# Decode attention on one core: two heads share each K and V tile with 64 KB rows, one V buffer, an in-place fold and block-diagonal probabilities

## The chip, the cores and the metric

The kernel runs on one core of a Trainium2 chip. The time is the device time of one execution, in microseconds (us). "The profile" is one profiled execution; its span (from the first to the last instruction) is some 1.7 us shorter than the device time of the same execution.

## The reference

One token goes through a block with adaptive layer norm: attention over a long cache, then a gated feed-forward network (FFN). What matters is the attention: 32 query heads, each with its own K and V of 16,384 keys by 128, all bfloat16.

```python
B, Sq, D = (1, 1, 640)
Hq, Hkv, Sk, Dh = (32, 32, 16384, 128)
...
h = _layernorm(x, axis=-1) * (1 + ca) + sa
q = (h @ wq).reshape(B, Sq, Hq, Dh).transpose(0, 2, 1, 3)
scores = jnp.einsum('bhqd,bhkd->bhqk', q, k) * Dh ** (-0.5)
p = _softmax(scores, axis=-1)
o = jnp.einsum('bhqk,bhkd->bhqd', p, v)
x = x + ga * (o.transpose(0, 2, 1, 3).reshape(B, Sq, Hq * Dh) @ wo)
# ... then the FFN: w_gate, w_up [640, 1728], w_down [1728, 640]
```

K and V are 268 MB of the 290 MB that one execution reads, and every byte is used once.

## The kernel before

Every head's K (4 MB) is laid over 128 partitions, so each partition gets 128 keys: one contiguous row of 32 KB. VectorE multiplies it by the query (spread over all partitions) and adds the two halves of the 128 products into `f1`; TensorE, with an identity matrix, adds further, down to eight partial sums a key, in PSUM (the memory that TensorE writes to); VectorE reduces those eight. Then maximum, exp, and PV (the probabilities times V) on TensorE. Two K slots and two V slots take turns. Every operation has a position number, and each engine runs its operations in the order of these numbers.

```python
kring = sb("kring", [128, 2, TT, 128], BF16)      # TT = 128 keys a partition
vring = sb("vring", [128, 2, TT, 128], BF16)
f1 = sb("f1", [128, TT, 64], BF16)
kv = lambda t, h: t[0, h].rearrange("(p t) d -> p t d", p=128)
# ... for each head h; s2 = h % 2; NH = 2 chunks, TH = 64
d_k[h] = plan.dma(qpos["k", h], kring[:, s2], kv(A_k, h), ("k", s2),
                  deps=[o_fold1[h - 2]] if h >= 2 else [], ...)
vdeps = [o_pvlast[h - 2]] if h >= 2 else [o_mod_a, o_mod_b, o_gbrmm]
# ... for each chunk c
o_mult[h] = op(DVE, base + 6.5 * c, ... tensor_tensor(out=ks, in0=ks, in1=qb, op=ALU.mult), ...)
o_fold1[h] = op(DVE, base + 6.5 * c + 4.4, ... tensor_tensor(
    out=f1h, in0=ks[:, :, 0:64], in1=ks[:, :, 64:128], op=ALU.add), ...)
# ... f_fold: eight matmuls with the identity; red, max, exp; then
def f_pv(e, s2=s2, sp=sp):
    for j in range(NJ):
        q4 = 32 * (j % 4)
        r = e.matmul(acc_ps[s2][q4:q4 + 32, :], lhsT=P_sb[:, sp, 4 * j:4 * j + 32],
                     rhs=vring[:, s2, 4 * j:4 * j + 4, :]..., start=(j < 4), stop=(j >= NJ - 4))
# ... acc (PSUM to SBUF), diag (picks the diagonal blocks out), on (divides by the sum), wo (output projection)
```

## Time and profile before

| | kernel before |
|---|---|
| time, median of 3 runs | 688.63 us (688.21 to 688.77) |
| span of the profiled run | 686.8 us |
| first transfer packet / last weight packet lands | 1.8 us / 682.7 us |
| DMA rate, 150 to 640 us | 430 GB/s |

First come lines of the page of the kernel before: the busy time of the engines, then the share of busy DMA engines (in tenths) and the GB/s in 40 equal slices, and the packets.

```profile
span 686.8 us, 7505 instructions
PE 350.9 (51%) x3320; PEld 174.7 (25%) x3320; DVE 482.4 (70%) x251; ACT 81.5 (12%) x308; POOL 51.3 (7%) x75
DMA  9999999999999999999999999999999999999996
DMA packets 12845, 290.96 MB, mean 424 GB/s; under 512 B 1354, under 2 KB 2060, under 8 KB 3724
```

No engine but the DMA is above 70%, and the DMA row is full until the last slice. The table of busy time by stretch says the same with numbers; its last two columns are the DMA share and GB/s.

```profile
core 0: us, PE busy (x) PEld busy (x) DVE busy (x) ACT busy (x) POOL busy (x), PEclk, DMA share, GB/s
50.00:100.00 50.00, 26.83 (x179) 11.56 (x179) 42.52 (x21) 6.61 (x25) 11.44 (x6) 0.71 1.00 430
100.00:105.00 5.00, 4.38 (x41) 1.55 (x40) 4.13 (x3) 0.60 (x1) 0.00 (x0) 0.82 0.99 426
105.00:110.00 5.00, 2.82 (x36) 2.13 (x34) 3.17 (x3) 1.52 (x6) 1.68 (x2) 0.86 0.97 419
150.00:640.00 490.00, 251.39 (x2061) 118.94 (x2061) 374.37 (x176) 58.89 (x221) 30.69 (x50) 0.69 1.00 430
```

The two big VectorE operations, from the groups of instructions (the numbers after the bar are total us and mean ns):

```profile
L425 DVE TENSOR_TENSOR kring<-kring,qbc_sb 128x8192 bf16<-128x8192 bf16 x64 | 283.0, 4422 | 94.4 <-DMA kring<-in_A_k_cache_dram 70.0
L427 DVE TENSOR_TENSOR f<-kring 128x4096 bf16<-128x4096 bf16 x64 | 146.7, 2292 | 2.2
```

And the end: first the chain of waits (start, duration, what), then three lines of the timeline.

```profile
653.02 28.72 DMA kring<-in_B_w_down_dram
681.79 0.73 PE psb L594 x16
684.44 0.33 DVE o_row L604
```

```profile
671.43 0.17 DVE L549 TENSOR_TENSOR h_col<-tt,mod_col 128x5 bf16<-128x5 f32 x1
676.77 2.24 PE L563 MATMUL psb<-h_col,wreg 128*128 128x1 bf16 x70 [2.52 <-DMA wreg<-in_B_w_up_dram]
684.79 0.63 SPq L71 DMA_DIRECT2D out_dram<-o_row  x1
```

The FFN's input `h_col` is ready at 671.4 us, but the "up" matmuls still wait 2.5 us for their weights, and after that the down weights are the last wait. The kernel is limited by transfers from the first packet to the last; only about 4 us at the end and 2 at the start are something else.

### The profile page before, as it was taken

Reading aid. Unit: us, or ns where it says so; the run is one execution under the profiler, and the core shown is the slowest. Engines: PE = TensorE matmul, PEld = TensorE weight load, DVE = VectorE, ACT = ScalarE, POOL = GpSimd, SP = SyncE. Lnnn points to the kernel's source line nnn. Section 1 sums busy time; section 2 is a strip of 40 time slices with the busy share of each in tenths; the row PEclk is TensorE's granted clock in tenths of the full one; section 3 lists DMA queues with packets and bytes.
Section 4 is the critical chain, followed back from the end, with each engine's and each line's share of the span. In section 5 each row is a group of like instructions: output and inputs, shape, how many; then the busy total and the mean of one; then the engine's idle time right before and its main releaser. Section 6 shows DMA issues by size and latency. Waiting matters only on the chain.

```text
span 686.8 us, 7505 instructions
## 1 busy us (share of the span) xinstructions
PE 350.9 (51%) x3320; PEld 174.7 (25%) x3320; DVE 482.4 (70%) x251; ACT 81.5 (12%) x308; POOL 51.3 (7%) x75
## 2 busy tenths in 40 slices
PE   1525665545655344655445456553445455565464
PEld 1501222222222122322122222321222122232143
DVE  0078888767778777768887677787777788877811
ACT  0100111111100011110111111100111011110010
POOL 0002222000000000000000000000000222200000
PEclk9997777666677676676777666775776566666755
DMA  9999999999999999999999999999999999999996
GB/s 387 409 434 427 433 434 435 426 433 430 431 420 441 430 427 428 430 429 434 431 433 430 430 427 431 427 434 428 433 436 418 438 428 428 428 429 430 425 421 238
DMA packets 12845, 290.96 MB, mean 424 GB/s; under 512 B 1354, under 2 KB 2060, under 8 KB 3724
## 3 DMA queue, kind: packets, MB, share of 16 engines
q1 hardware_dynamic: 12808, 290.48, 98.9%
q8 instruction: 26, 0.43, 0.3%
q14 instruction: 7, 0.06, 0.0%
q10 hardware_dynamic: 4, 0.00, 0.0%
HBM read 290.47 MB, written 0.00 MB: 423 GB/s over the span
## 4 chain that ended last, share of the span: by engine, by line
DMA 51%; DVE 41%; PE 6%; ACT 1%; issue 1%; SPq 1%; POOL 0%; DVEq 0%
DMA kring<-in_A_k_cache_dram 46%; DVE kring L425 26%; DVE f L427 14%; DMA kring<-in_B_w_down_dram 4%; PE psb L435 3%; PE psb L485 1%; SPq L71 1%; DVE S_sb L439 0%; ACT P_sb L450 0%; PE psb L465 0%; PE psb L594 0%; ACT R_sb L408 0%; POOL gm L446 0%; ACT qbc_sb L414 0%; PE psb L411 0%
## 5 line engine op out<-in xcount | busy, mean ns | idle before, releaser
L425 DVE TENSOR_TENSOR kring<-kring,qbc_sb 128x8192 bf16<-128x8192 bf16 x64 | 283.0, 4422 | 94.4 <-DMA kring<-in_A_k_cache_dram 70.0
L435 PE MATMUL psb<-f,ident 128*128 128x512 bf16 x512 | 177.6, 510 | 255.0 <-DVE f L427 254.9
L427 DVE TENSOR_TENSOR f<-kring 128x4096 bf16<-128x4096 bf16 x64 | 146.7, 2292 | 2.2
L435 PEld LDWEIGHTS psb<-f,ident 128*128 128x128 bf16 x512 | 56.4, 121 | 355.4 <-DVE f L427 275.2
L439 DVE TENSOR_REDUCE S_sb<-psb 128x64 f32<-128x512 f32 x64 | 44.0, 688 | 52.4 <-PE psb L435 52.4
L465 PE MATMUL psb<-vring,P_sb 128*32 128x512 bf16 x992 | 75.0, 455 | 9.2 <-DMA vring<-in_A_v_cache_dram 9.2
L485 PEld LDWEIGHTS psb<-sel,acc_sb 128*32 128x32 f32 (+1 forms) x920 | 59.8, 158 | 13.8 <-issue 11.9
L485 PE MATMUL psb<-sel,acc_sb 128*32 128x1 f32 (+1 forms) x920 | 62.0, 201 | 0.7 <-ACT acc_sb L470 0.7
L470 ACT ACTIVATE acc_sb<-psb 128x512 f32<-128x512 f32 x31 | 18.5, 597 | 355.7 <-PE psb L465 355.7
L446 POOL PARTITION_ALL_REDUCE gm<-pm x32 | 11.2, 351 | 533.4 <-DVE pm L443 515.3
L465 PEld LDWEIGHTS psb<-vring,P_sb 128*32 128x32 bf16 x992 | 26.6, 111 | 64.6 <-DMA vring<-in_A_v_cache_dram 28.1
L453 POOL PARTITION_ALL_REDUCE Ls<-rs x32 | 37.3, 1164 | 48.8 <-ACT P_sb L450 48.8
L411 PE MATMUL psb<-R_sb,ones_bf 128*128 128x128 bf16 x32 | 8.5, 266 | 35.8 <-ACT R_sb L408 35.2
L504 ACT ACTIVATE On<-psb,rl 32x4 bf16<-32x4 f32 (+1 forms) x32 | 8.2, 256 | 125.4 <-PE psb L485 120.7
L411 PEld LDWEIGHTS psb<-R_sb,ones_bf 128*128 128x128 bf16 x32 | 3.2, 101 | 39.8 <-ACT R_sb L408 39.8
L450 ACT ACTIVATE P_sb<-S_sb,nb 128x128 bf16<-128x128 f32 x32 | 12.9, 402 | 1.0
L408 ACT ACTIVATE R_sb<-ident,q_r 128x128 bf16<-128x128 bf16 x32 | 12.4, 387 | 0.0
L448 ACT ACTIVATE nb<-gm 128x1 f32<-128x1 f32 x32 | 6.4, 199 | 40.6 <-POOL gm L446 40.1
L540 DVE TENSOR_TENSOR tt<-attn_bf,mod_col 128x5 f32<-128x5 bf16 x1 | 0.2, 167 | 14.8 <-ACT attn_bf L539 14.8
L414 ACT ACTIVATE qbc_sb<-psb 128x128 bf16<-128x128 f32 x32 | 8.9, 277 | 11.5 <-PE psb L411 11.5
L512 PE MATMUL psb<-On,woring 128*128 128x1 bf16 x160 | 8.1, 179 | 3.9 <-ACT On L504 3.9
L443 DVE TENSOR_REDUCE pm<-S_sb 128x1 f32<-128x128 f32 x32 | 9.2, 286 | 1.1
(72 smaller groups left out, 85.6 us busy)
## 6 DMA issues: line engine op xcount, KB each, us to landing
kring<-in_A_k_cache_dram SPq DMA_DIRECT2D x32, 4096.0 KB, 25.4
vring<-in_A_v_cache_dram SPq DMA_DIRECT2D x31, 4096.0 KB, 35.3
wreg<-in_A_wq_dram SPq DMA_DIRECT2D x1, 5120.0 KB, 26.9
woring<-in_A_wo_dram SPq DMA_DIRECT2D x8, 640.0 KB, 26.6
vring<-in_w_mod_dram SPq DMA_DIRECT2D x1, 4800.0 KB, 14.3
vring<-in_A_v_cache_dram SPq DMA_DIRECT2D x4, 1024.0 KB, 12.5
wreg<-in_B_w_gate_dram SPq DMA_DIRECT2D x1, 2160.0 KB, 19.8
wreg<-in_B_w_up_dram SPq DMA_DIRECT2D x1, 2160.0 KB, 24.6
```

What stands on the lines that cost most here:

```text
L408: o_R[h] = op(ACT, base - 15.0 if h > 0 else 2.5, lambda e, h=h, s2=s2: e.activation(out=R_sb[:, s2], in_=ident[:], func=ACTF.Copy, scale= ...
L411: o_qbcmm[h] = op(PE, base - 14.8 if h > 0 else 2.7, lambda e, s2=s2: e.matmul(qbc_ps[s2], lhsT=ones_bf[:], rhs=R_sb[:, s2], start=True, s ...
L425: o_mult[h] = op(DVE, base + 6.5 * c, lambda e, ks=ks, qb=qb: e.tensor_tensor(out=ks, in0=ks, in1=qb, op=ALU.mult), deps=[d_k[h], o_qbc[h] ...
L427: o_fold1[h] = op(DVE, base + 6.5 * c + 4.4, lambda e, ks=ks, f1h=f1h: e.tensor_tensor(out=f1h, in0=ks[:, :, 0:64], in1=ks[:, :, 64:128], ...
L435: r = e.matmul(sh, lhsT=ident[:], rhs=f1h[:, :, GC * m:GC * (m + 1)], start=(m == 0), stop=(m == n - 1))
L439: reds.append(op(DVE, base + 15.0 + c, lambda e, s2=s2, sh=sh, c=c: e.tensor_reduce(out=S_sb[:, s2, c * TH:(c + 1) * TH], in_=sh, axis=AX. ...
L446: o_gm[h] = op(POOL, base + 17.3, lambda e, h=h: e.partition_all_reduce(gm[:, h:h + 1], pm[:, h:h + 1], channels=128, reduce_op=bass.bass_ ...
L450: o_exp[h] = op(ACT, base + 18.2, lambda e, h=h, s2=s2, sp=sp: e.activation(out=P_sb[:, sp, 0:TT], in_=S_sb[:, s2], func=ACTF.Exp, scale=S ...
L453: o_L[h] = op(POOL, base + 18.6, lambda e, h=h: e.partition_all_reduce(Ls[:, h:h + 1], rs[:, h:h + 1], channels=128, reduce_op=bass.bass_i ...
L465: r = e.matmul(acc_ps[s2][q4:q4 + 32, :], lhsT=P_sb[:, sp, 4 * j:4 * j + 32], rhs=vring[:, s2, 4 * j:4 * j + 4, :].rearrange("p a d -> p ( ...
L470: o_acc[h] = op(ACT, vbase + 3.0, lambda e, s2=s2: e.activation(out=acc_sb[:, s2, :], in_=acc_ps[s2][:], func=ACTF.Copy), deps=[o_pvlast[h ...
L485: r = e.matmul(dst, lhsT=blk, rhs=sel[:, i:i + 1], start=(i == 0), stop=(i == 3))
```

## The change

The intent: two heads (a pair) are one tile of 8 MB, 64 partitions a head, so each partition's row is one run of 64 KB, with half as many packets and half as many softmax chains. Beside two such K slots the kernel keeps one V buffer only; the fold writes into the K tile itself, the early and late weights borrow the tiles, and PV is cut into two halves that are placed among the next pair's folds. Each half of the partitions belongs to another head, so the probabilities are written as a block-diagonal matrix (columns of the other head are zero), and one PV pass serves both heads. The core of the diff:

```diff
-    kv = lambda t, h: t[0, h].rearrange("(p t) d -> p t d", p=128)
+    kv = lambda t, i: t[0, 2 * i:2 * i + 2].rearrange("h (p t) d -> (h p) t d", p=64)
-    vring = sb("vring", [128, 2, TT, 128], BF16)
-    f1 = sb("f1", [128, TT, 64], BF16)
+    kring = sb("kring", [128, 2, TP, 128], BF16)      # TP = 256
+    vbuf = sb("vbuf", [128, TP, 128], BF16)
 ... (wm_v, wq_v and the FFN weights are views of vbuf and of K slot 1)
+    order += [("k", NI - 2), ("k", NI - 1), ("v", NI - 3), ("v", NI - 2), ("wo", NI // 2 - 1), ("v", NI - 1)]
+    vt = [kring[:, 0] if i == NI - 2 else vbuf for i in range(NI)]
+    op_pos = []                                       # positions of PV half a, PV half b, diag
+    for i in range(NI):
+        nxt = T0 + (i + 1) * PERIOD                   # start of the next pair; its folds are at +6.9, +13.9, +20.9, +27.9
+        if i < NI - 3:
+            op_pos.append((nxt + 14.0, nxt + 21.0, nxt + 28.0))
+        elif i == NI - 3:
+            op_pos.append((nxt + PERIOD - 6.0, nxt + PERIOD - 5.0, nxt + PERIOD - 4.0))
 ... (the last two pairs)
+    o_f1 = op(DVE, base + 7.0 * c + 4.4, ... tensor_tensor(
+        out=ks[:, :, 0:64], in0=ks[:, :, 0:64], in1=ks[:, :, 64:128], op=ALU.add), deps=[o_mult[i]], ...)
+    o_exp[i] = op(ACT, ..., out=P_sb[half[b], sp, 0:2 * TP].rearrange("p (t b) -> p b t", b=2)[:, b, :], ...)
+    vdeps = [...] if i == 0 else [o_fold[i][-1]] if i == NI - 2 else [o_pvlast[i - 2 if last else i - 1]]
+    o_pva = op(PE, pva, lambda e, f=f_pv, j=jc[0]: f(e, 0, j), deps=[o_exp[i], d_v[i][0], ...])
+    o_pvb = op(PE, pvb, lambda e, f=f_pv, j=jc: f(e, j[0], j[1]), deps=[o_pva, ...])
```

## The prediction

> **What bounds the kernel now.** The DMA engines. The 40-slice page shows DMA at 9 in all slices but the last; the table of busy time by stretch gives a DMA share of 1.00 and 430 GB/s over 60 to 640 us. VectorE is busy 70%, TensorE 51%; neither sets the pace, as the queue is never empty (a K load takes 25.4 us to land, 9.7 of them its own transfer). The chain of waits says "DMA K 46%, VectorE 41%" only because it hops to whatever freed a buffer. Sum: 1.8 us to the first packet, 680 of transfers, 4.5 from the last weight packet to the end.
>
> **What the change does to that bound.** Bytes stay (290 MB); the row per partition goes from 32 KB to 64 KB. Packet records of the trace: 8 KB takes 312 ns, 17 KB 647, 32 KB 1215, 40 KB 1514: a line of 0.0367 ns/B (435 GB/s over 16 engines) plus about 10 ns a packet. The Trainium skill, "DMA: Bandwidth & Descriptors", "Where 436 GB/s comes from", gives 435 GB/s as the ceiling of the SBUF ports; the trace agrees, so only those 10 ns can be won. About 250 packets per engine disappear: an estimated 2.7 us, if a 64 KB row moves as one packet (three chances in four); nothing if it is cut in two.
>
> **What it removes off the critical path.** Half of the max and all-reduce bubbles (VectorE waits 4.9 us per head between last fold and next multiply; then about 5.5 per pair). VectorE per pair: 4 x (4.42 + 2.29) + 4 x 0.7 + 2 x 0.45 + wait = about 34 us against 39 of DMA. The in-place fold keeps 16-bit unit-step runs, so I expect 2.29 us again (the skill's "VectorE: DVE Perf Modes", "What auto-detection actually checks", asks for that). PV, diagonal and fold matmuls keep count and shape. All hidden.
>
> **What it adds.** One V buffer, and PV cut in two among the next pair's folds. In steady state the next V load is issued 30 us after its pair's multiply starts, 9 us before the queue runs dry: no loss. Only at the start is it late: the first K tile is twice as long, so VectorE starts at 47.6 us instead of 37.9, pair 1 at about 81, and the second half of PV of pair 0, after three folds of pair 1, ends at about 108.5; but the K tile of pair 2 has landed at 106.6. The queue is empty for about 3 us, once. By pair 3 VectorE has caught up. At the end the transfers keep their order, FFN weights last; the last PV chunk ends near 667.5 us as before and the up weights still land later, so the tail stays.
>
> **Sum.** 688.6 - 2.7 x 0.75 + 3 = about 689.5 us. Range 684 to 695. Within 2%: 0.92; faster 0.02; slower 0.06.
>
> **What would show it.** Packets of 65,536 bytes at about 2420 ns (else 32 KB at 1215). About 432 GB/s from 150 to 640 us. A stretch of 2 to 4 us without DMA near 106 to 110 us, the queue waiting for PV matmuls. 64 multiplies at 4.42 and 64 folds at 2.29 us.
>
> **What would make it wrong.** 64 KB rows moving slower (engines reading the same memory channels); the in-place fold losing its fast mode (4.5 us each: VectorE 43 us a pair, slower by about 60 us in all); stalls of the single V buffer in steady state (each counts 16 times); no stall at the start (then 686).

## The result, and the profile after

| | before | changed |
|---|---|---|
| time, median of 4 runs | 688.61 us | 689.53 us (688.09 to 689.80) |
| ratio to before, 95% interval | | 1.001 (0.9993 to 1.0027): the same |
| span of the profiled run | 686.8 us | 687.6 us |
| last weight packet lands | 682.7 us | 681.7 us |

Ratios here are the mean time of one kernel's runs over the mean of the other's runs of the same rounds, so they are not quite the ratios of the medians that are quoted. The total is what was predicted, to 0.1 us. But a sum can be right with wrong terms, so each term was looked up.

The page of the changed kernel, the same lines:

```profile
span 687.6 us, 7232 instructions
PE 352.1 (51%) x3264; PEld 169.6 (25%) x3264; DVE 484.0 (70%) x251; ACT 68.4 (10%) x245; POOL 26.5 (4%) x45
DMA  9999999999999999999999999999999999999995
DMA packets 8089, 290.92 MB, mean 423 GB/s; under 512 B 826, under 2 KB 1532, under 8 KB 3196
```

The packets fell by 37%, the bytes stayed. The mean rate did not rise, and the table of stretches shows why:

```profile
core 0: us, PE busy (x) PEld busy (x) DVE busy (x) ACT busy (x) POOL busy (x), PEclk, DMA share, GB/s
50.00:100.00 50.00, 22.78 (x82) 7.10 (x82) 45.67 (x21) 2.22 (x9) 3.56 (x2) 0.69 1.00 434
100.00:105.00 5.00, 2.80 (x28) 1.14 (x28) 5.00 (x3) 0.00 (x0) 0.00 (x0) 1.00 0.94 406
105.00:110.00 5.00, 1.48 (x22) 0.53 (x15) 4.97 (x3) 1.17 (x3) 0.00 (x0) 1.00 0.60 210
150.00:640.00 490.00, 257.19 (x2091) 119.02 (x2092) 372.29 (x172) 50.60 (x178) 14.97 (x25) 0.66 1.00 432
```

From 150 to 640 us the rate is 432 GB/s where it was 430, but from 105 to 110 us the DMA share falls to 0.60. (This view counts a packet whole in the stretch where it starts, so the share shows the place of a gap and only roughly its size.) The packet records of the trace give the first part exactly (ns of one packet):

| bytes of one packet | before | changed |
|---|---|---|
| 16,384 | | 612 median |
| 32,768 | 1215 median, 1218.8 mean (8064 of them) | 1214.5 median (128) |
| 65,536 | | 2420 median, 2427.0 mean (3968) |

Two packets of 32 KB take 2 x 1218.8 = 2437.6 ns and one of 64 KB takes 2427.0, so a pair of rows gains 10.6 ns. Each of the 16 engines moves 3968 / 16 = 248 of them: 2.6 us.

The second part is the gap. The timeline of the changed kernel, the transfer queue and TensorE around 100 us:

```profile
79.07 0.33 SPq L71 DMA_DIRECT2D kring<-in_A_k_cache_dram  x1
106.11 0.33 SPq L71 DMA_DIRECT2D vbuf<-in_A_v_cache_dram  x1
111.51 0.33 SPq L71 DMA_DIRECT2D kring<-in_A_k_cache_dram  x1
```

```profile
98.21 1.91 PE L482 MATMUL psb<-vbuf,P_sb 128*32 128x512 bf16 x32
102.32 1.90 PE L445 MATMUL psb<-kring,ident 128*128 128x512 bf16 x8 [2.20 <-DVE kring L438]
104.15 1.91 PE L482 MATMUL psb<-vbuf,P_sb 128*32 128x512 bf16 x32
```

The second half of PV of pair 0 (104.15 us) stands behind the third fold of pair 1 (102.32 us). When it is done, V of pair 1 may be loaded into the only V buffer: issued at 106.11 us, first packet at 107.06. The K tile in front of it had ended, engine by engine, between 104.8 and 106.6 us. So the 16 engines idled 1.7 us on average, but all of them at once only 0.45 us. This uneven end is what the Trainium skill leads one to expect ("DMA: Bandwidth & Descriptors", "Why a DMA increments its semaphore by 16 and not by 1": the engines of one transfer finish independently); the 1.8 us between first and last is this trace's number.

VectorE kept its two operations at their speed; the in-place fold costs the same 2292 ns:

```profile
L436 DVE TENSOR_TENSOR kring<-kring,qbc_sb 128x8192 bf16<-128x8192 bf16 x64 | 282.7, 4418 | 119.0 <-DMA kring<-in_A_k_cache_dram 111.4
L438 DVE TENSOR_TENSOR kring<-kring 128x4096 bf16<-128x4096 bf16 x64 | 146.7, 2292 | 2.2
```

The third part is at the end. The chain of waits of the changed kernel, from its last 50 us:

```profile
651.88 3.00 PE psb L482 x25
661.20 0.62 ACT P_sb L462 x2
663.95 3.57 PE psb L482 x32
676.43 0.18 DVE h_col L573
676.66 4.44 PE psb L587 x140
685.20 0.33 DVE o_row L628
```

There is no transfer in it any more; the last one of the whole chain is the V tile of pair 13, which landed at 625.4 us. The FFN's input is ready at 676.4 us, 5.0 us later than before; gate and up then run in one piece (140 matmuls, 4.44 us), as all their weights are there:

```profile
676.43 0.17 DVE L573 TENSOR_TENSOR h_col<-tt,mod_col 128x5 bf16<-128x5 f32 x1
676.66 4.43 PE L587 MATMUL psb<-h_col,kring 128*128 128x1 bf16 x140 [1.87 <-DVE h_col L573]
685.55 0.63 SPq L71 DMA_DIRECT2D out_dram<-o_row  x1
```

The transfers ended 1.0 us earlier than before and the output went out 0.8 us later: the tail grew by 1.8 us. Followed back, the delay starts here:

```profile
625.42 6.13 PE L482 MATMUL psb<-vbuf,P_sb 128*32 128x512 bf16 x64 [6.91 <-DMA vbuf<-in_A_v_cache_dram]
632.26 3.79 PE L508 MATMUL psb<-sel,acc_sb 128*32 128x1 f32 x64 [0.71 <-ACT acc_sb L491]
637.48 5.08 PE L445 MATMUL psb<-kring,ident 128*128 128x512 bf16 x16
640.88 0.69 DVE L449 TENSOR_REDUCE S_sb<-psb 128x64 f32<-128x512 f32 x1 [6.53 <-PE psb L445]
```

On TensorE, PV of pair 13 waits for its V tile, then its diagonal picks and the output projection follow, and only after all of that the first fold of pair 15 (the first eight of the 16 matmuls from 637.48 us), whose operands had been ready since 627.6 us (the fold on VectorE started at 625.39 and took 2.29). VectorE waits 6.5 us for that fold, and the exp of the last pair comes at 661.2 us, after its V had begun to land.

So my theory after the result: **A**, three terms nearly cancel: -2.6 us of packets, a gap at the start, a longer tail. Its rival **B**: nothing of this counts, the two kernels are equal because the bytes are equal and row size and small gaps do not matter; the early end and late end are noise. For the tail alone there is a second rival, **C**: the last pair's own work is longer (two heads, 64 matmuls and two outputs at the end).

### The profile page after: what moved, and what is told of

It reads as the page before. It is cut to its first block, busy times and chain, and to the rows that moved or that the text cites. A ratio compares the mean times of both kernels' runs of the same rounds, so it can differ in the third digit from the quotient of the medians.

```text
span 687.6 us, 7232 instructions
## 1 busy us (share of the span) xinstructions
PE 352.1 (51%) x3264; PEld 169.6 (25%) x3264; DVE 484.0 (70%) x251; ACT 68.4 (10%) x245; POOL 26.5 (4%) x45
## 4 chain that ended last, share of the span: by engine, by line
DMA 46%; DVE 36%; PE 12%; issue 3%; ACT 2%; another core or an unknown queue 1%; SPq 0%; POOL 0%; POOLq 0%; DVEq 0%
DMA kring<-in_A_k_cache_dram 38%; DVE kring L436 23%; DVE kring L438 10%; DMA vbuf<-in_A_v_cache_dram 7%; PE psb L445 4%; PE psb L508 3%; PE psb L482 2%; DVE S_sb L449 2%; PE psb L535 1%; ACT P_sb L462 1%; PE psb L587 1%; PE psb L618 0%; ACT On L527 0%; SPq L71 0%
## 5 line engine op out<-in xcount | busy, mean ns | idle before, releaser
L445 PE MATMUL psb<-kring,ident 128*128 128x512 bf16 x512 | 185.3, 528 | 251.5 <-DVE kring L438 251.4
L445 PEld LDWEIGHTS psb<-kring,ident 128*128 128x128 bf16 x512 | 58.3, 124 | 370.3 <-DVE kring L438 277.2
L438 DVE TENSOR_TENSOR kring<-kring 128x4096 bf16<-128x4096 bf16 x64 | 146.7, 2292 | 2.2
L482 PE MATMUL psb<-vbuf,P_sb 128*32 128x512 bf16 x944 | 76.9, 482 | 34.7 <-DMA vbuf<-in_A_v_cache_dram 34.5
L508 PEld LDWEIGHTS psb<-sel,acc_sb 128*32 128x32 f32 x896 | 51.8, 156 | 6.7 <-issue 5.5
L508 PE MATMUL psb<-sel,acc_sb 128*32 128x1 f32 x896 | 53.0, 199 | 0.7 <-ACT acc_sb L491 0.7
L482 PEld LDWEIGHTS psb<-vbuf,P_sb 128*32 128x32 bf16 x944 | 27.3, 114 | 82.6 <-issue 42.9
L466 POOL PARTITION_ALL_REDUCE Ls<-rs x16 | 17.5, 1092 | 55.4 <-ACT P_sb L462 55.4
L462 ACT ACTIVATE P_sb<-S_sb,nb 64x256 bf16<-64x256 f32 x32 | 18.5, 577 | 0.7
L454 DVE TENSOR_REDUCE pm<-S_sb 64x1 f32<-64x256 f32 x32 | 13.2, 414 | 0.8
```

What stands on the lines that cost most here:

```text
L438: o_f1 = op(DVE, base + 7.0 * c + 4.4, lambda e, ks=ks: e.tensor_tensor(out=ks[:, :, 0:64], in0=ks[:, :, 0:64], in1=ks[:, :, 64:128], op=A ...
L445: r = e.matmul(sh, lhsT=ident[:], rhs=ks[:, :, GC * m:GC * (m + 1)], start=(m == 0), stop=(m == n - 1))
L454: o_mx = op(DVE, eb + 0.1 * b, lambda e, i=i, b=b: e.tensor_reduce(out=pm[half[b], 2 * i + b:2 * i + b + 1], in_=S_sb[half[b]], axis=AX.X, ...
L462: o_exp[i] = op(ACT, eb + 0.6 + 0.1 * b, lambda e, i=i, b=b, sp=sp: e.activation(out=P_sb[half[b], sp, 0:2 * TP].rearrange("p (t b) -> p b ...
L466: o_L[i] = op(POOL, eb + 0.9, lambda e, hc=hc: e.partition_all_reduce(Ls[:, hc], rs[:, hc], channels=128, reduce_op=bass.bass_isa.ReduceOp ...
L482: r = e.matmul(acc_ps[s2][q4:q4 + 32, :], lhsT=P_sb[:, sp, 8 * j:8 * j + 32], rhs=vt[i][:, 4 * j:4 * j + 4, :].rearrange("p a d -> p (a d) ...
```

## The experiments

All outputs are right. The runs of one group used the same chip and shared the rounds of the kernel before, whose medians there were 688.61, 688.60 and 688.54 us.

| run | median (range) us | ratio to before (95%) |
|---|---|---|
| e1_rows32 | 691.08 (690.17 to 692.09) | 1.0036 (1.0024 to 1.0049) |
| e2_tail | 687.88 (687.51 to 688.06) | 0.9989 (0.9976 to 1.0001) |
| e3_start | 686.75 (685.99 to 688.52) | 0.9977 (0.9965 to 0.9990) |
| e4_both | 686.75 (685.96 to 687.62) | 0.9974 (0.9960 to 0.9987) |
| e5_after_again | 689.08 (687.72 to 690.10) | 1.0008 (0.9996 to 1.0021) |
| e6_start_again | 686.57 (685.99 to 687.38) | 0.9973 (0.9960 to 0.9985) |
| e7_late | 697.41 (696.64 to 697.84) | 1.0125 (1.0110 to 1.0141) |
| e8_before_rows16 | 693.38 (693.16 to 693.70) | 1.0070 (1.0057 to 1.0083) |
| e9_both_again | 687.32 (685.82 to 687.55) | 0.9978 (0.9965 to 0.9990) |
| e10_early2 | 685.90 (685.52 to 686.98) | 0.9964 (0.9952 to 0.9977) |
| e11_qbc_first | 685.98 (685.64 to 686.18) | 0.9964 (0.9951 to 0.9978) |

All of them are within 2% of the kernel before; the differences of 1 to 8 us below are read from the medians, five runs each (four for e7_late). The changed kernel itself is taken at 689.1 us (e5_after_again, beside e6 to e8); for the first group, measured on another chip, the equal times of the kernel before are the bridge.

**e1_rows32: the packets alone.** The changed kernel, with each tile fetched as two transfers whose rows are 32 KB.

```diff
-            d_k[i] = plan.dma(qpos["k", i], kring[:, s2], kv(A_k, i), ("k", s2), deps=kdeps, ...)
+            d_k[i] = [plan.dma(qpos["k", i] + 0.01 * n, kring[:, s2, TT * n:TT * (n + 1), :],
+                               kv(A_k, i)[:, TT * n:TT * (n + 1), :], ("k", s2, n), deps=kdeps, ...) for n in range(2)]
 ... (V the same; multiplies and PV wait for both)
```

> The changed kernel with each 8 MB K and V tile fetched as two transfers of 32 KB rows instead of one of 64 KB rows; every wait still waits for both. Theory A (three terms cancel: fewer packets give back 2.6 us, the late first V load costs 1.7, the later end costs 1.8): the packet gain goes away, so 2.6 us slower than the changed kernel, about 692 us; 32 KB packets at 1215 ns, 430 GB/s. Theory B (nothing changed because the bytes are the same and rows do not matter at this size): 689.5 us, unchanged.

Measured: 691.08 us, 2.0 us slower than the changed kernel. The last weight packet landed at 684.2 us instead of 681.7, which is 2.5 us later, as expected; the output followed only 1.0 us later in the profiled runs (686.56 against 685.55). The path to the output runs through V of pair 13, and that came 2.5 us later too (its PV starts at 627.90 instead of 625.42 us); the other 1.5 us were made up behind it on TensorE, where this PV took 5.26 instead of 6.13 us and later ones less as well.

```profile
627.90 5.26 PE L483 MATMUL psb<-vbuf,P_sb 128*32 128x512 bf16 x64 [7.21 <-DMA vbuf<-in_A_v_cache_dram]
```

Over the 248 more packets an engine, 2.5 us are 10 ns a packet, the 2.0 us of the medians 8 ns. B is refuted for the rows.

**e8_before_rows16: the same cost in the other kernel.** The kernel before, each tile fetched as two transfers with 16 KB rows.

```diff
-            d_k[h] = plan.dma(qpos["k", h], kring[:, s2], kv(A_k, h), ("k", s2), ...)
+            d_k[h] = [plan.dma(qpos["k", h] + 0.01 * n, kring[:, s2, 64 * n:64 * n + 64, :], kv(A_k, h)[:, 64 * n:64 * n + 64, :], ("k", s2, n), ...) for n in range(2)]
 ... (V the same; multiplies and PV wait for both)
```

> The kernel before with each K and V tile fetched as two transfers of 16 KB rows, 504 more packets per engine. Theory A (every packet costs a fixed time beside its bytes): from the 16 KB packets already seen (611 ns) twice 611 less 1215 is 7 ns a row, 3.5 us slower in all, about 692 us; at most 5. Theory B (rows do not matter at this size): unchanged, 688.6.

Measured: 693.38 us, 4.8 us slower, the upper end of what was expected. Over about 504 more packets an engine that is 4.8 / 504 = 9.5 ns a packet, in a kernel whose queue never runs dry. One rival has to be looked at: both runs double the number of transfers too, so a cost for each transfer would give the same times. The packet records decide for the packets: by the medians in the table above, two of 16 KB take 2 x 612 - 1214.5 = 9.5 ns more than one of 32 KB, and two of 32 KB 2 x 1214.5 - 2420 = 9 ns more than one of 64 KB, and a median is not moved by the few packets at the ends of transfers. Together with e1 this settles the packet term: 8 to 10 ns for each packet, at rows of 16, 32 and 64 KB alike.

**e2_tail: the end alone.** The diagonal picks of pair 13 and what follows them stand behind the first fold of pair 15 instead of before it.

```diff
-                op_pos.append((nxt + PERIOD - 6.0, nxt + PERIOD - 5.0, nxt + PERIOD - 4.0))
+                op_pos.append((nxt + PERIOD - 6.0, nxt + PERIOD - 5.0, nxt + PERIOD + 7.0))
```

> The changed kernel with the diagonal picks and the output projection of pair 13 moved on TensorE from before the first fold of pair 15 to after it. Theory A: VectorE's 6.5 us wait for that fold goes, the exp of the last pair comes about 6 us earlier (near 656 instead of 662 us), gate and up start near 672.6 instead of 676.7, the end falls again to the last weight packet, and the time drops 1.8 us, to 687.7. Theory C (the later end comes from the last pair's own work, two heads' PV chunk, two outputs): exp comes earlier but the end stays, 689.5.

Measured: 687.88 us, 1.2 us less than the changed kernel (1.6 less than its first measurement); the ranges of the single runs just overlap (687.51 to 688.06 against 687.72 to 690.10), so it is the trace that carries the reading. In its trace the reduction that had started at 640.88 us runs at 634.18, without a wait, the exp at 653.3 instead of 661.2, and transfers are the last wait again. Its timeline and its chain of waits:

```profile
634.18 0.68 DVE L449 TENSOR_REDUCE S_sb<-psb 128x64 f32<-128x512 f32 x1
672.32 0.17 DVE L573 TENSOR_TENSOR h_col<-tt,mod_col 128x5 bf16<-128x5 f32 x1
676.68 2.25 PE L587 MATMUL psb<-h_col,kring 128*128 128x1 bf16 x70 [1.89 <-DMA kring<-in_B_w_up_dram]
683.75 0.63 SPq L71 DMA_DIRECT2D out_dram<-o_row  x1
```

```profile
652.10 28.61 DMA kring<-in_B_w_down_dram
680.76 0.73 PE psb L618 x14
```

The last weight packet landed at 681.6 us as in the changed kernel, and the output went out 1.8 us earlier (683.75 against 685.55). C is refuted: the last pair's own work is unchanged, and it fits.

**e3_start and e6_start_again: the gap alone.** Both halves of PV of pair 0 right after the second fold of pair 1.

```diff
+            if i == 0:
+                op_pos.append((nxt + 14.0, nxt + 14.1, nxt + 28.0))
-            if i < NI - 3:
+            elif i < NI - 3:
```

> The changed kernel with both halves of PV of pair 0 put after the second fold of pair 1 (the second half came after the third). Theory A: the second V load is issued at about 102 instead of 106.1 us, before the K tile ahead of it has landed (106.6), the 1.7 us of idle DMA engines between 100 and 120 us go, and the time drops by 1.7 us, to 687.8. Theory B: such a gap at the start is made up later, 689.5.

> The kernel of e3_start again beside the unaltered changed kernel. In e3_start the median fell 2.8 us against the first measurement, but in the profiled runs the last weight packet came only 0.8 us earlier: of the 16 DMA engines, those that had finished early idled 1.8 us at 105 to 107 us, the last to finish only 0.45 us. Theory A1 (the time follows the slowest DMA engine): 0.5 to 1.2 us off against the same-chip time of the changed kernel. Theory A2 (it follows the mean idle time of the engines): 1.7 us off. Neither explains 2.8; if that comes again, something else is also changed.

Measured: 686.75 us, and again 686.57 beside the unaltered kernel's 689.08: 2.5 us off. V of pair 1 is issued at 102.76 us, and no moment is left at which all engines idle. The timeline of e6_start_again:

```profile
102.76 0.33 SPq L71 DMA_DIRECT2D vbuf<-in_A_v_cache_dram  x1
113.50 0.33 SPq L71 DMA_DIRECT2D kring<-in_A_k_cache_dram  x1
```

B is refuted for the gap. The size is a miss: 0.5 to 1.2 us (A1) is too little, and 1.7 us (A2) is less than the 2.5 that came off. In the two profiled runs the last weight packet came 1.2 us earlier (680.8 against 681.9), the V tile of pair 13, on which the late tail hangs, 1.3 us earlier (624.05 against 625.36), and `h_col` 2.0 us earlier (674.22 against 676.23), since the 64 PV matmuls behind that V tile took 5.59 instead of 6.05 us and later ones gained as well. So part of the gain came through the tail and through TensorE, which does not repeat the same work in the same time: these 64 matmuls took 6.13, 6.05, 5.59 and 6.61 us in the traces of the changed kernel, e5, e6 and e3, and the granted clock from 624 to 631 us was 0.55, 0.57, 0.73 and 0.56 in them. Nor does the start move mend the tail by itself: in e3_start, the same kernel as e6_start_again, the profiled run was the slowest of five (688.52 us), and it had 3.8 us from the last weight packet to the output, as the changed kernel has, where e6_start_again had 2.6. How much of the 2.5 us belongs to the tail is not settled.

**e7_late: more of the same gap.** The opposite: the second half of PV of pair 0 after the fourth fold of pair 1.

```diff
+            if i == 0:
+                op_pos.append((nxt + 14.0, nxt + 27.95, nxt + 28.0))
-            if i < NI - 3:
+            elif i < NI - 3:
 ... (the copy of pair 0's PV result on ScalarE moved forward, which would otherwise deadlock)
```

> The opposite of e3_start: the second half of PV of pair 0 after the fourth fold of pair 1, so that the second V load is issued at about 113.4 us instead of 106.1. Theory A: all 16 engines idle 7.3 us more, once, and nothing later makes it up: the time rises by 7.3 us, to 696.8. Theory B (a gap at the start is caught up by the slack of later stages): less than 2 us more.

Measured: 697.41 us, 8.3 us slower. V of pair 1 was issued later than I had reckoned:

```profile
115.44 0.33 SPq L71 DMA_DIRECT2D vbuf<-in_A_v_cache_dram  x1
115.81 0.43 SPq L71 DMA_DIRECT2D kring<-in_A_k_cache_dram  x1
```

That is 9.3 us after the 106.11 of the changed kernel; all engines idled 9.65 us where it had been 0.45, and the last weight packet came 9.3 us later. The time rose by less, 8.3 us; in the profiled runs a part of that is a tail shorter by 0.7 us (2.7 us from the last weight packet to the output, against 3.4 in e5_after_again). Nothing in the next 550 us makes the gap in the transfers good: that is shown for a gap of this size.

**e4_both and e9_both_again: both moves.** The two edits above together.

> Both moves together. Theory A: the two costs are independent, 3.5 us off, 686.0 us; against the kernel before that is 2.6 us faster, what the saved packets are worth. Theory B: no more than 1 us off.

> The kernel of e4_both again, as the yardstick for the two beside it: 686.75 us expected, between 686 and 688. Its trace showed one more small gap, 0.5 us of idle DMA engines at 144 us, at the load of V of pair 2.

Measured: 686.75 and 687.32 us. That is about 2 us off where 3.5 were expected, and no better than the start move alone. The chain of waits ends in a transfer again, so the tail is mended here too; but in the trace of e6_start_again the tail had been only about 0.4 us too long (its output went out at 683.32 us, in e4_both at 682.89), so there was little left to gain. I took a further gap for another part: in e4_both the engines idled 0.5 us on average at 144 us, before V of pair 2. That is not shown: in the trace of e9_both_again, the same kernel, they did not idle there (0.6 us near 640 us instead), and it was no faster.

**e10_early2 and e11_qbc_first.** Pair 1's PV gets the same early place (e10); then, besides, the diagonal picks stand behind the matmul that spreads the next query (e11).

```diff
-            if i == 0:
+            if i < 2:
                 op_pos.append((nxt + 14.0, nxt + 14.1, nxt + 28.0))
 ... and for e11 only:
-                op_pos.append((nxt + 14.0, nxt + 14.1, nxt + 28.0))
+                op_pos.append((nxt + 14.0, nxt + 14.1, nxt + 28.3))
-                op_pos.append((nxt + 14.0, nxt + 21.0, nxt + 28.0))
+                op_pos.append((nxt + 14.0, nxt + 21.0, nxt + 28.3))
```

> e4_both with both halves of PV put after the second fold also for pair 1. Theory A (every gap of the transfers at the start is paid in full): V of pair 2 is issued at about 138.5 instead of 142.3 us, the 0.5 us of idle DMA at 144 us go, 0.5 us off: 686.3. Theory B (the start has no more to give): unchanged.

> e10_early2 with the diagonal picks of each pair put on TensorE after the matmul that spreads the next query instead of before it. In the changed kernel VectorE waits 2.8 us for that query copy in each of the first pairs. Theory A (DMA alone sets the pace, VectorE has slack): VectorE's wait goes and the time stays, within 0.3 us. Theory D (VectorE's waits are on the path): 2 to 8 us off.

Measured: 685.90 and 685.98 us. e10 is 1.4 us below e9_both_again by the medians (0.9 by the means), more than the 0.5 expected, and their ranges overlap. The reason that was expected does not carry this gain: V of pair 2 was issued earlier, at 139.32 us, and the engines do not idle at 144 us, but they did not in the trace of e9_both_again either. Why e10 is faster than e9 stays open. With e11 it is the fastest of all: 2.6 us below the kernel before, about what the saved packets were reckoned at. In its trace the last weight packet lands at 680.2 us, 2.5 us earlier than before the change. e11 took VectorE's waits for the query copy from 10.3 to 3.9 us in all and moved the time by nothing (its waits for K rose from 103.9 to 109.9 us instead): these waits are not on the path, and D is refuted. So with three changes of order on TensorE the kernel gains about what its packets save. That the account closes to the tenth of a us is not shown.

## Why the prediction was right

- **Transfers bound the kernel, and only the time per packet can be won.** Right. 65,536-byte packets came out at 2420 ns and the rate at 432 GB/s, both as predicted. The skill's ceiling of 435 GB/s for the SBUF ports ("DMA: Bandwidth & Descriptors", "Where 436 GB/s comes from") agrees to 1%, while the limit of about 358 GB/s that the same section sets for transfers from HBM was passed here, with one core at work. The term was 2.6 us, against 2.0 in the sum, which had been discounted for the chance that the rows would be split.
- **In-place fold.** Right: 2292 ns before and after, as "VectorE: DVE Perf Modes", "What auto-detection actually checks", leads one to expect of 16-bit operands with unit step; and VectorE starts pair 1 at 81.6 us (predicted 81).
- **The gap at the start.** The mechanism, the place and its single occurrence were right; the size was off. Predicted were 108.5 us for the end of PV of pair 0 and about 3 us of empty queue. It ended at 106.1, as both halves took 1.91 us at full clock where I had reckoned with the slower 2.5 to 3.6 us of the trace before; all engines idled 0.45 us at once, 1.7 on average. Taking it away gave 2.5 us, a part of it through the tail.
- **"The tail stays."** This step was wrong. I had followed the transfers to the end, found them in the same order, and taken the last PV chunk to end at 667.5 us. It ended at 672.3, since on TensorE a PV that had to wait for V of pair 13 stood before a fold of pair 15. The runs showed 1.8 us more from last weight to output in the profile, of which e2_tail took 1.2 to 1.6 us off the time.
- The sum was right to 0.1 us because the packets gave 0.6 us more than predicted and the gap, by mean idle time, took 1.3 us less (1.7 against 3), while the tail took 1.8 us more. The agreement is partly luck. The experiments weigh the terms a little differently (packets 2.0 us, gap 2.5, tail 1.2 to 1.6), and gap and tail are not independent: both moves together gave about 2 us.

What stays open: the spread of the changed kernel's runs (687.7 to 690.1 us, against 688.3 to 689.2 for the kernel before in the same rounds). With the tail mended it was 0.6 us in e2_tail, but 1.5 to 1.7 us in e4_both, e9 and e10, and again 0.5 us in e11. One pair of traces shows TensorE's part: e3_start and e6_start_again are the same kernel, their last weight packets landed 0.2 us apart and their outputs went out 1.4 us apart. For the kernels with the mended tail it is argued, not shown, that TensorE's varying speed and the uneven ends of the DMA engines make the spread. Also open are why e10 is faster than e9, and how the 2.5 us of the start move are made up.

## What to carry to other kernels

In a kernel that is bound by transfers, reckon a change as bytes times the slope plus packets times the cost of one, then look for every place where the queue runs dry: here a gap of 9 us at the start cost 8.3 us at the end, 550 us later. One buffer instead of two is free only if the work that frees it comes early enough in its engine's order; so read that order, not only the dependencies. When a total agrees with its prediction, check the terms: here a gain of 2 to 2.6 us was hidden behind delays that two orders on TensorE made, and three changed positions gave it back.

## What the Trainium skill lacked or had wrong

- "DMA: Bandwidth & Descriptors", "Why small descriptors are slow (HBM only)", gives each packet a fixed cost and works it out for 256 bytes. The page has about 10.5 ns a packet for a transfer of 4 KB, but no passage says what a packet costs beside its bytes when rows are long. That was 8 to 10 ns at rows of 16, 32 and 64 KB (e8: 9.5 ns; e1: 8 to 10), worth 2.0 to 2.6 us of 688.6 in a queue that is almost never empty.
- The same page names no transfer time by row size for rows of this length. The trace has 612 ns for 16 KB, 1215 for 32 KB and 2420 for 64 KB, so a 64 KB row moves as one packet.
- No page gives a figure for the spread among the 16 engines of one transfer. Here the ends of one 8 MB tile lay 1.8 us apart, and an empty queue cost the engines 1.7 us on average, but all of them at once only 0.45 us.
- The same page, "Latency and other measured facts", gives about 600 ns to the first byte for this kind of transfer and does not say from which moment. The first packet after an empty queue started 0.95 us after the issuing instruction began (106.11 to 107.06 us), which is 0.62 us after it ended, so the figure fits if it is counted from the end.
